# Query products on 64x64 float32 quarters, and attention steps done for two chunks at a time

## The chip, the cores and the metric

The kernel runs on one core of one Trainium2 chip. The metric is the device time of one execution in microseconds (us). Three executions of the kernel before were timed; a further one was profiled. The engines are named as the profile names them: PE is TensorE (matmuls), PEld its weight loads, DVE is VectorE, ACT is ScalarE, POOL is GpSimd, and SP is SyncE, whose queue starts nearly all DMAs here.

## What is computed

A linear attention without softmax, with an RMS norm, feeds two feed-forward layers. All arrays are float32 in the reference.

```
def _attn_ref(q, k, v, g_norm):                      # 8 batches, 8 heads, 576 rows, 64 wide
    kv = np.einsum('bhsd,bhse->bhde', k, v)
    out = np.einsum('bhsd,bhde->bhse', q, kv)
    rms = np.sqrt(np.mean(out * out, axis=-1, keepdims=True) + 1e-06)
    return out / rms * g_norm
x = transpose(attn, (0, 2, 1, 3)).reshape(4608, 512)
h = max(x @ w1, x @ w2, x @ w3)                      # 512 -> 768
x = h @ w_out                                        # 768 -> 512
h = x @ w_in                                         # 512 -> 2048
out = (s * relu(h)**2 + b) @ w_out2                  # 2048 -> 512
```

The weights of the first feed-forward layer reach the kernel as 64-bit floats, which it turns into float32 itself.

## The kernel before

**Stages.** The rows go through in nine groups of 512: the first 512 rows of each of the 8 batches, and as a ninth group the 64 left-over rows of all 8 batches. For group `j`, TensorE forms 18 sums of 12 matmuls each (`g1_part`, lines L96 to L98, PSUM tiles `g`), three for each of the 6 blocks of 128 hidden columns, whose maximum is kept; then 4 sums of 18 matmuls (`g2_mm`, the same lines, read `<-h,w_o`). The factor 12 is four chunks of 128 of the 512 columns, times three: a float32 matmul is done as three matmuls of split operands in fp32r (`mm3`). A split writes the high part on ACT (L92) and the low part, source minus high part, on DVE or POOL (L93). Attention of batch `j + 1` is worked out beside group `j`, so its matmuls stand between those of group `j`. Two Strassen-like stages for the second feed-forward layer follow from about 747 us on; the change does not touch them.

**Attention of a batch.** The 8 heads are handled in 4 pairs `p`: a pair is heads `p` and `p + 4`, one in partitions 0 to 63, the other in 64 to 127. `kv_mm` (L243) sums k times v for a pair in plain float32, into two halves of 64 PSUM partitions. `kv_diag` copies the sums into `kvf`, a 128x128 matrix for each pair with the two heads' 64x64 blocks on its diagonal and zeros elsewhere. `q_turn` transposes the pair's queries. `o_mm` multiplies: in batch 0 in one plain float32 matmul of 512 columns (L291), in the later batches in three fp32r matmuls (L295 to L297), for which `kv_diag` splits `kvf` and `q_split` the queries; one small float32 matmul of 64 columns (L300, tile `orps`) takes the left-over rows. `o_out` copies and squares the product (ACT); `ms_mm` sums the squares over a head (L325 in batch 0, L328 and L329 later, PSUM tile `ms`, one buffer); `ms_ln` takes ln, exp and a square on ACT; `ms_newton` does a Newton step of three DVE operations (L342 to L344); `x_split` splits the normalized chunk into `xh` and `xl`.

**The opening.** In group 0 nothing can be overlapped with an earlier group. The 18 blocks of w1 to w3 and 6 of w_out are loaded (`conv_load`, L149), turned to float32 (`conv_unpack`, `conv_sum`: L161 to L166 and L171, 3 operations on DVE, 3 on ACT, 1 on POOL) and split. Three staging buffers hold the raw blocks. The first four sums (`g` 0 to 3) of group 0 are formed chunk by chunk, as the chunks arrive.

**What sets the order.** Each step is entered with a position (`at(position, step, ...)`), and the steps are issued by position. From position 20 on, SP and PE keep that order; before it only SP does, and PE's order in the opening, like that of DVE, ACT and POOL all through, is set by a scheduler when the program is built. On the chip each engine works through its list strictly in order.

Of the kernel before, what the change touches and what calls it, by code (L numbers as in the profile page):

```python
# [9 lines left out]
F32 = mybir.dt.float32  # L10
F32R = mybir.dt.float32r
# [18 lines left out]
def attention_max_ffn_relu2_ffn(ctx: ExitStack, tc, q, k, v, g_norm, w1, w2, w3, wo, wi, w2o, s, b, out):  # L30
# [109 lines left out]

    st = {}
# [85 lines left out]
    def load_kv(bb, p):  # L227
        for nm, src in (("k", k), ("v", v)):
            tag = (nm, 2) if bb or p < 2 else ("o", NP)
            t = st[nm, bb, p] = at_.tile([P, 2, C, D], F32, tag=tag[0], bufs=tag[1], name=f"{nm}_{bb}_{p}")  # L230
# [3 lines left out]
    def kv_mm(bb, p):  # L234
        if p == 0:
            st["kvps", bb] = psa.tile([P, NP, D], F32, tag="kv", name=f"kvps_{bb}")
# [8 lines left out]
    def kv_out(bb):  # L245
        t = st["kvc", bb] = at_.tile([P, NP, D], F32, tag="kvc", bufs=4, name=f"kvc_{bb}")
        act(out=t, in_=st.pop(("kvps", bb)), func=AF.Copy)
# [6 lines left out]
    def kv_diag(bb):  # L254
# [9 lines left out]
        st["kvhl"] = (kvh, kvl)  # L264
# [15 lines left out]
    def q_split(bb, p):  # L280
        t = st["qt", p]
        qh = at_.tile([P, N], F32R, tag="qh", name=f"qh_{bb}_{p}")
        ql = at_.tile([P, N], F32R, tag="ql", name=f"ql_{bb}_{p}")
        split(qh, ql, t[:, :N], nc.vector)
        st["q", p] = (qh, ql)

    def o_mm(bb, p):
        ps = st["ops", p] = psa.tile([P, N], F32, tag="o", name=f"ops_{bb}_{p}")
        mm = nc.tensor.matmul
        if bb == 0:  # L290
            mm(ps, lhsT=kvf[:, p], rhs=st["qt", p][:, :N], start=True, stop=True)  # L291
        else:
            kvh, kvl = st["kvhl"]
            qh, ql = st["q", p]
# [3 lines left out]
        if p == 0:  # L298
# [580 lines left out]
```

## Time and profile before

| | us |
|---|---|
| three timed runs, median (lowest to highest) | 1456.11 (1453.32 to 1458.19) |
| profiled execution, first to last instruction | 1453.9 |
| PE busy in it | 1396.9 |
| DVE, ACT, POOL busy | 951.2, 813.8, 332.7 |
| group 0 (from the start to the first matmul of group 1) | 156.6 |
| groups 1 to 8 (to about 747 us) | 590 |
| the rest | 707 |

The profile gives no time of the profiled execution beyond its span. The span lies 2.2 us under the median of the timed runs and inside their spread of 4.9 us. PE's busy time counts a matmul from its start to a modelled end, so a row of matmuls without a gap shows as 100% busy; what one matmul costs in such a row is the step from its start to the next one's.

### The profile page before, as it was taken

The numbers are of one execution on the slowest core, as the hardware profiler recorded it, in microseconds if no ns is written. First come the engines' busy times: TensorE is split into PE (matmuls) and PEld (weight loads), VectorE is DVE, ScalarE is ACT, GpSimd is POOL, SyncE is SP. The second block draws the span as 40 slices with busy tenths as digits, with TensorE's granted clock in tenths as the row PEclk, the third lists the DMA queues.
The fourth block names the chain that finished last, engine by engine and source line by source line (L and its number), as shares of the span: only waits on it lengthen the run. The fifth ranks groups of instructions, "written<-read, shape, count | busy, mean of one in ns | idle before, by whom it ended". The sixth has DMA issues, their size and how long they took to land. (4 is left out here: it accounts for less than half of the span.)

```text
span 1453.9 us, 19580 instructions
## 1 busy us (share of the span) xinstructions
PE 1396.9 (96%) x6860; PEld 1145.0 (79%) x6860; DVE 951.2 (65%) x1439; ACT 813.8 (56%) x1454; POOL 332.7 (23%) x238
## 2 busy tenths in 40 slices
PE   4689999999999999999999999999999999999997
PEld 2467888888878788888878778988788888888887
DVE  4899473646364636446466765756877888888785
ACT  5776454445353545443365646647676666656565
POOL 1334242324232324331100000000002414141412
PEclk9789999999999999999999999999999999999999
DMA  9986244435364742213135464453676444454541
GB/s 195 198 207 106 76 65 111 111 117 102 127 91 124 113 123 58 80 29 116 65 124 202 162 230 178 142 203 127 217 265 231 132 146 174 152 175 148 176 135 40
DMA packets 229459, 202.63 MB, mean 139 GB/s; under 512 B 126320, under 2 KB 179568, under 8 KB 227184
## 3 DMA queue, kind: packets, MB, share of 16 engines
q1 hardware_dynamic: 229200, 201.11, 48.9%
q8 instruction: 54, 0.88, 0.3%
q14 instruction: 45, 0.37, 0.1%
q10 hardware_dynamic: 160, 0.26, 0.0%
HBM read 126.88 MB, written 74.45 MB: 138 GB/s over the span
## 5 line engine op out<-in xcount | busy, mean ns | idle before, releaser
L97 PE MATMUL g<-xl,w_w 128*128 128x512 f32 x648 | 255.9, 395 | 3.8 <-POOL xl L93 3.8
L96 PE MATMUL g<-xh,w_w 128*128 128x512 f32 x648 | 257.4, 400 | 0.2 <-ACT xh L92 0.2
L98 PE MATMUL g<-xh,w_w 128*128 128x512 f32 x648 | 255.6, 395 | 0.0
L92 ACT ACTIVATE zx<-z 128x512 fp32r<-128x512 f32 (+1 forms) x280 | 161.2, 586 | 123.5 <-PE zs_a L707 35.7
L629 PE MATMUL ps_a<-x_q,w_q 128*128 128x512 f32 (+1 forms) x960 | 211.1, 371 | 2.8 <-DVE cs L537 1.7
L707 PE MATMUL zs_a<-zx,w_q 128*128 128x512 f32 (+1 forms) x960 | 203.7, 369 | 0.6 <-POOL zx L93 0.3
L93 POOL TENSOR_TENSOR zx<-z,zx 128x512 fp32r<-128x512 f32 (+1 forms) x46 | 63.3, 1376 | 593.8 <-DMA gd<-cs 381.4
L629 PEld LDWEIGHTS ps_a<-x_q,w_q 128*128 128x128 f32 x960 | 167.2, 188 | 38.0 <-DVE cs L537 3.4
L93 DVE TENSOR_TENSOR zx<-z,zx 128x512 fp32r<-128x512 f32 (+1 forms) x234 | 170.6, 746 | 34.8 <-ACT zx L92 34.3
L707 PEld LDWEIGHTS zs_a<-zx,w_q 128*128 128x128 f32 x960 | 167.8, 188 | 31.9 <-POOL zx L93 0.7
L97 PEld LDWEIGHTS g<-xl,w_w 128*128 128x128 f32 x648 | 123.3, 190 | 29.7 <-POOL xl L93 4.2
L96 PEld LDWEIGHTS g<-xh,w_w 128*128 128x128 f32 x648 | 123.2, 191 | 26.8 <-issue 1.0
L98 PEld LDWEIGHTS g<-xh,w_w 128*128 128x128 f32 x648 | 123.2, 190 | 26.3
L171 POOL TENSOR_TENSOR tr_ctr<-tr_ctr,gc_cgc 128x512 int32<-128x512 int32 x42 | 56.0, 1333 | 232.4 <-DVE gc_cgc L166 169.8
L629 PE MATMUL ps_b<-x_q,w_q 128*128 128x512 f32 (+1 forms) x480 | 107.6, 372 | 1.1 <-ACT cs L640 1.0
L707 PE MATMUL zs_b<-zx,w_q 128*128 128x512 f32 (+1 forms) x480 | 103.8, 371 | 2.2 <-DVE zx L93 2.2
L372 DVE TENSOR_TENSOR h<-g,h 128x512 f32<-128x512 f32 x108 | 73.9, 684 | 42.9 <-PE g L98 42.4
L707 PEld LDWEIGHTS zs_b<-zx,w_q 128*128 128x128 f32 x480 | 83.9, 188 | 19.1 <-DVE zx L93 3.4
L629 PEld LDWEIGHTS ps_b<-x_q,w_q 128*128 128x128 f32 x480 | 83.8, 188 | 18.9 <-ACT cs L640 1.8
L96 PE MATMUL g<-h,w_o 128*128 128x512 f32 x216 | 85.7, 397 | 0.0
L162 ACT ACTIVATE tr_ctr<-raw_craw 128x512 int32<-128x512 uint32 x42 | 28.1, 669 | 102.1 <-DMA wd<-tr_ctr 86.1
L97 PE MATMUL g<-h,w_o 128*128 128x512 f32 x216 | 84.6, 392 | 0.0
(160 smaller groups left out, 2268.3 us busy)
## 6 DMA issues: line engine op xcount, KB each, us to landing
z<-gd SPq DMA_DIRECT2D x64, 512.0 KB
gd<-cs SPq DMA_DIRECT2D x96, 256.0 KB
z<-gd SPq DMA_DIRECT2D x48, 256.0 KB
x1d<-x SPq DMA_DIRECT2D x36, 256.0 KB
k<-in_k_dram SPq DMA_DIRECT2D x32, 256.0 KB
v<-in_v_dram SPq DMA_DIRECT2D x32, 256.0 KB
raw_craw<-in_moe_w_in_dram SPq DMA_DIRECT2D x16, 512.0 KB
wd<-tr_ctr SPq DMA_DIRECT2D x32, 256.0 KB
```

Of the source, the lines that this page charges most:

```text
L92: act(out=hi, in_=src, func=AF.Copy)
L93: eng.tensor_tensor(out=lo, in0=src, in1=hi.bitcast(F32), op=ALU.subtract)
L96: nc.tensor.matmul(ps, lhsT=w[:, 0, sl], rhs=xh, start=first, stop=False)
L97: nc.tensor.matmul(ps, lhsT=w[:, 0, sl], rhs=xl, start=False, stop=False)
L98: nc.tensor.matmul(ps, lhsT=w[:, 1, sl], rhs=xh, start=False, stop=last)
L162: act(out=r, in_=w32[:, :, 0], func=AF.Copy, scale=2.0 ** -29)
L171: nc.gpsimd.tensor_tensor(out=t, in0=t, in1=g.bitcast(I32), op=ALU.add)
L372: nc.vector.tensor_tensor(out=st["h", m], in0=ps, in1=st["h", m], op=ALU.max)
L629: nc.tensor.matmul(ps, lhsT=w[:, a, c], rhs=x[:, b_], start=new and k == 0 and e == 0, stop=k == HK - 1 and e == 2, skip_group_check=True)
L707: nc.tensor.matmul(ps, lhsT=w[:, a, c], rhs=x[:, b_, :n], start=new and k_ == 0 and e == 0, stop=k_ == 3 and e == 2, skip_group_check=True)
```

## The change

`o_mm` multiplies in plain float32 in all batches, on quarters of the array: for each head of a pair a 64x64 block of `kvf` is the stationary operand, with 64 partitions of queries. Two pairs, a unit `u`, share a PSUM tile of two banks: pair `2u` goes to output partitions 0 to 63 and pair `2u + 1` to 64 to 127, and the head decides the bank. A chunk now holds heads `4h + 2u` and `4h + 2u + 1`, so the blocks of w1 to w3 are loaded by one DMA of 128 partitions instead of two of 64, and chunks are taken in the order 0, 2, 1, 3 of the weights. The splits of queries and of `kvf` are gone. Copy, square, split of squares, the last two Newton operations and the split into `xh`, `xl` work on two chunks (1024 columns) at once; the sums of squares, ln, exp and the first Newton operation stay at 512. The left-over rows and the k-v sums share one PSUM bank (`kvor`). The low halves of chunks 0 and 1 in the opening move from POOL to DVE; in later groups POOL does the first unit's, DVE the second's.

```diff
     def w1_src(n):
-        return [(h * D, D, w[h * NP * D:(h + 1) * NP * D, :].rearrange("(k d) c -> d k c", d=D)) for h in range(2)]
+        return [(0, P, w.rearrange("(k p) c -> p k c", p=P))]
...
     def kv_diag(bb):
             act(out=kvf[sl, :, sl], in_=t[sl], func=AF.Copy)
-        if bb == 0:
-            return
-        kvh = at_.tile([P, NP, P], F32R, tag="kvh", name=f"kvh_{bb}")
-        kvl = at_.tile([P, NP, P], F32R, tag="kvl", name=f"kvl_{bb}")
-        split(kvh, kvl, kvf, nc.vector)
...
-    def q_split(bb, p):
-        split(qh, ql, t[:, :N], nc.vector)
-    def o_mm(bb, p):
-        ps = st["ops", p] = psa.tile([P, N], F32, tag="o", name=f"ops_{bb}_{p}")
-            mm(ps, lhsT=kvh[:, p], rhs=qh, start=True, stop=False)
-            mm(ps, lhsT=kvh[:, p], rhs=ql, start=False, stop=False)
-            mm(ps, lhsT=kvl[:, p], rhs=qh, start=False, stop=True)
-        mm(st["orps"][:, p], lhsT=kvf[:, p], rhs=st["qt", p][:, N:], start=True, stop=True)
+    def o_mm(bb, u, pp):
+        if pp[0] == 2 * u:
+            st["ops", u] = psa.tile([P, 2, N], F32, tag="o", name=f"ops_{bb}_{u}")
+        for h in range(2):
+            for p in pp:
+                sl = slice(h * D, (h + 1) * D)
+                nc.tensor.matmul(st["ops", u][p % 2 * D:(p % 2 + 1) * D, h], lhsT=kvf[sl, p, sl],
+                                 rhs=st["qt", p][sl, :N], start=True, stop=True)
+        for h in range(2):
+            for p in pp:
+                nc.tensor.matmul(kvor[p % 2 * D:(p % 2 + 1) * D, 1, 2 * u + h], lhsT=kvf[:, p, h * D:(h + 1) * D],
+                                 rhs=st["qt", p][:, N:], start=True, stop=True)
...
-    def ms_newton(bb, p):
-        stt(out=u, in0=st["ms", p], scalar=EPS, in1=u, op0=ALU.add, op1=ALU.mult)
+    def ms_newton(bb, c):
+        u = st["yu", c // 2][1][:, c % 2]
+        stt(out=u, in0=st["ms", c], scalar=EPS, in1=u, op0=ALU.add, op1=ALU.mult)
+    def o_norm(bb, u_):
         stt(out=u, in0=u, scalar=-3.0, in1=y, op0=ALU.add, op1=ALU.mult)
         stt(out=o, in0=o, scalar=g_sb, in1=u, op0=ALU.mult, op1=ALU.mult)
...
     for p in range(NP):
-        at(us(a + 2.7), o_out, 0, p)
-        at(us(a + 6), x_split, 0, p, nc.gpsimd if p < 2 else nc.vector)
+        if p % 2:
+            at(us(a + 2.7), o_out, 0, u)
+            at(us(a + 7), x_split, 0, u, nc.vector)
```

**The block in a later group.** PE's rows in batch 5's attention, between sums 12 and 13 of group 4, before: the product of one pair (`ops`) in three matmuls, the pair's left-over rows (`orps`) in one. There are four such blocks for a batch.

```order
L98 MATMUL g_4_12_3457<-xh_2997,w_w_698 128x512
L295 MATMUL ops_3_3479<-qh_3_3426,kvh_3173 128x512
L296 MATMUL ops_3_3479<-ql_3_3427,kvh_3173 128x512
L297 MATMUL ops_3_3479<-qh_3_3426,kvl_3174 128x512
L300 MATMUL orps_3238<-qt_3_3392,kvf 128x64
L96 MATMUL g_4_13_3495<-xh_2997,w_w_750 128x512
```

The same rows after, between sums 8 and 9 of group 4, for two pairs:

```order
L98 MATMUL g_4_8_3084<-xh_2761,w_w_521 128x512
L285 MATMUL ops_1_3107<-qt_2_3057,kvf 64x512
L285 MATMUL ops_1_3107<-qt_3_3082,kvf 64x512
L285 MATMUL ops_1_3107<-qt_2_3057,kvf 64x512
L285 MATMUL ops_1_3107<-qt_3_3082,kvf 64x512
L289 MATMUL kvor<-qt_2_3057,kvf 64x64
L289 MATMUL kvor<-qt_3_3082,kvf 64x64
L289 MATMUL kvor<-qt_2_3057,kvf 64x64
L289 MATMUL kvor<-qt_3_3082,kvf 64x64
L96 MATMUL g_4_9_3116<-xh_2761,w_w_543 128x512
```

Two blocks of four matmuls with 128 output partitions have become one block of eight with 64 each, and there are two such blocks for a batch.

**DVE in the opening.** DVE's rows around the low half of the last chunk of batch 0 (`xl<-o_3`), before. The tiles `gc`, `tr` and `raw` belong to the turning of weight blocks, `w_w` to their split.

```order
L165 SCALAR_TENSOR_TENSOR tr_o_586<-raw_o_547,tr_o_586 128x512
L161 TENSOR_SCALAR gc_o_621<-raw_o_570 128x512
L93 TENSOR_TENSOR kvl_556<-kvf,kvh_555 128x512
L166 SCALAR_TENSOR_TENSOR gc_o_587<-raw_o_547,tr_o_586 128x512
L93 TENSOR_TENSOR w_w_550<-tr_o_538,w_w_550 128x512
L93 TENSOR_TENSOR xl_292<-o_3_420,xh_291 128x512
L93 TENSOR_TENSOR w_w_577<-tr_ctr,w_w_577 128x512
L165 SCALAR_TENSOR_TENSOR tr_o_620<-raw_o_570,tr_o_620 128x512
```

The same place after; `raw_o_591` is the 14th block here, and `xl<-o_1` holds the low halves of chunks 2 and 3.

```order
L339 SCALAR_TENSOR_TENSOR o_1_389<-o_1_389,g_sb,u_1_428 128x1024
L167 SCALAR_TENSOR_TENSOR gc_cgc<-raw_craw,tr_ctr 128x512
L274 STREAM_TRANSPOSE qt_2_744<-qraw_398 128x576
L274 STREAM_TRANSPOSE qt_3_801<-qraw_398 128x576
L162 TENSOR_SCALAR gc_o_670<-raw_o_591 128x512
L308 TENSOR_SCALAR sqh_0_687<-sq_0_629 128x1024
L166 SCALAR_TENSOR_TENSOR tr_o_669<-raw_o_591,tr_o_669 128x512
L93 TENSOR_TENSOR xl_325<-o_1_389,xh_324 128x1024
```

Before, the block begun just ahead of the low half (`raw_o_570`) is the 12th, and the first operation on the 14th comes 12 rows behind the low half; now it comes 3 rows ahead of it. ACT's list has the same turn: the first ACT operation on the 14th block now stands directly ahead of the high halves of chunks 2 and 3.

**PE in the opening.** PE's rows after, from the k-v sums of batch 2 (`v_2_580`) to the first low-half matmul of chunks 2 and 3:

```order
L245 MATMUL kvor<-v_2_580,k_2_578 64x64 x8
L245 MATMUL kvor<-vrem,krem 64x64 x2
L285 MATMUL ops_1_863<-qt_2_744,kvf 64x512
L96 MATMUL g_0_0_342<-xh_324,w_w_183 128x512
L96 MATMUL g_0_1_349<-xh_324,w_w_211 128x512
L96 MATMUL g_0_2_356<-xh_324,w_w_254 128x512
L96 MATMUL g_0_3_363<-xh_324,w_w_276 128x512
L285 MATMUL ops_1_863<-qt_3_801,kvf 64x512
L285 MATMUL ops_1_863<-qt_2_744,kvf 64x512
L285 MATMUL ops_1_863<-qt_3_801,kvf 64x512
L245 MATMUL kvor<-v_3_614,k_3_612 64x64 x8
L97 MATMUL g_0_0_342<-xl_325,w_w_183 128x512
```

Ahead of that low-half matmul now stand all four k-v sums of batch 2 and all of batch 1's products. Before, one k-v sum of batch 2 and the product of one pair of batch 1 stood ahead of it; three k-v sums and nine fp32r matmuls of three pairs came later.

## Rows read from the trace of the kernel before

**Rows 1.** By stretch, us busy: PE, PEld, DVE, ACT, POOL; then clock, DMA share, GB/s.

```profile
0.00:156.60 156.60, 115.21 (x660) 84.70 (x661) 119.86 (x174) 101.33 (x181) 52.07 (x39) 0.88 0.81 165
156.60:747.00 590.40, 588.20 (x2858) 481.51 (x2858) 309.94 (x439) 280.87 (x480) 172.60 (x121) 1.00 0.40 96
747.00:1454.00 707.00, 693.52 (x3345) 578.80 (x3343) 521.35 (x827) 431.61 (x794) 108.02 (x78) 1.00 0.50 170
...
78.40:158.00 79.60, 71.14 (x407) 56.87 (x406) 68.49 (x94) 52.37 (x94) 30.31 (x19) 0.94 0.59 130
```

**Rows 2.** What PE waited for, 78 to 160 us: us, times, longest.

```profile
PE ms L328 <- DVE u L342: 3.4, 1, 3.4
PE kvps L243 <- DMA vrem<-in_v_dram: 3.2, 1, 3.2
PE kvps L243 <- DMA v<-in_v_dram: 1.9, 1, 1.9
```

**Rows 3.** PE: start, us, operation; last of the first four sums, first of group 1.

```profile
78.06 0.40 PE L98 MATMUL g<-xh,w_w 128*128 128x512 f32 x1
...
156.64 0.39 PE L96 MATMUL g<-xh,w_w 128*128 128x512 f32 x1
```

**Rows 4.** By stretch, columns as in rows 1: behind two of the waits.

```profile
104.00:108.00 4.00, 4.00 (x16) 2.83 (x17) 4.00 (x8) 3.52 (x7) 0.98 (x1) 0.57 0.84 302
134.00:142.00 8.00, 6.08 (x15) 4.78 (x16) 7.16 (x10) 4.18 (x7) 1.99 (x2) 0.57 0.64 107
```

**Rows 5.** PE in order of time: one pair's k-v sums between full matmuls.

```profile
528.30 0.39 PE L96 MATMUL g<-h,w_o 128*128 128x512 f32 x1
...
528.75 0.39 PE L98 MATMUL g<-h,w_o 128*128 128x512 f32 x1
529.07 0.69 PE L243 MATMUL kvps<-v,k 128*64 128x64 f32 x16
529.58 0.29 PE L243 MATMUL kvps<-vrem,krem 128*64 128x64 f32 x4
...
530.14 0.39 PE L97 MATMUL g<-xl,w_w 128*128 128x512 f32 x1
```

**Rows 6.** PE in order of time: one pair's products.

```profile
569.16 0.39 PE L295 MATMUL ops<-qh,kvh 128*128 128x512 f32 x1
...
569.85 0.33 PE L300 MATMUL orps<-qt,kvf 128*128 128x64 f32 x2
...
570.30 0.40 PE L97 MATMUL g<-xl,w_w 128*128 128x512 f32 x1
```

**Rows 7.** Tile ops: duration in ns (min/median/max), first and last start, form.

```profile
L295 PE MATMUL ops<-qh,kvh x28: 391/391/774, 70.4 to 569.2; 128*128 128x512 f32 x28
L291 PE MATMUL ops<-qt,kvf x8: 592/1061/1222, 9.3 to 35.9; 128*128 128x512 f32 x8
```

**Rows 8.** DVE's groups to 156.6 us: count, busy us, mean ns, idle before.

```profile
L93 DVE TENSOR_TENSOR ql<-qt,qh 128x512 fp32r<-128x512 f32 x5 | 4.2, 839 | 0.0
...
L93 DVE TENSOR_TENSOR kvl<-kvf,kvh 128x512 fp32r<-128x512 f32 x2 | 1.4, 678 | 0.0
```

**Rows 9.** Groups by form over the whole span: busy us, mean ns, idle before.

```profile
L537 DVE TENSOR_TENSOR cs<-ps_a,cs 128x512 f32<-128x512 f32 x32 | 21.6, 686 | 3.7 <-PE ps_a L629 3.6
...
L537 DVE TENSOR_TENSOR cs<-ps_a,cs 128x256 f32<-128x256 f32 x8 | 3.0, 418 | 0.2 <-PE ps_a L629 0.2
```

**Rows 10.** DVE and ACT in order of time: last low half; 14th block's start.

```profile
73.28 1.77 DVE L93 TENSOR_TENSOR xl<-o,xh 128x512 fp32r<-128x512 f32 x1
...
83.37 0.67 ACT L162 ACTIVATE tr_o<-raw_o 128x512 int32<-128x512 uint32 x1 [2.36 <-DMA raw_o<-in_moe_w_dram]
```

**Rows 11.** Tile raw_o, ns: SP's start of a 64-partition load; a block's first DVE operation.

```profile
L149 SPq DMA_DIRECT2D raw_o<-in_moe_w_dram x24: 595/608/733, 11.7 to 96.6; - x24
...
L161 DVE TENSOR_SCALAR gc_o<-raw_o x12: 410/427/1379, 17.1 to 102.8; 128x512 uint16<-128x512 uint16 x12
```

**Rows 12.** The page: the span.

```profile
span 1453.9 us, 19580 instructions
```

More of the change, by code (lines that the diff above doesn't have):

```diff
@@ L139, in attention_max_ffn_relu2_ffn @@
         nc.gpsimd.memset(rems[nm], 0.0)
+    kvor = psa.tile([P, 2, NP, D], F32, name="kvor")
     st = {}
@@ L324, in ms_mm @@
+    def ms_mm(bb, c):
+        u, h = divmod(c, 2)
+        ps = st["ms", c] = psa.tile([P, N], F32, tag="ms", name=f"ms_{bb}_{c}")
         if bb == 0:
-            nc.tensor.matmul(ps, lhsT=onesf, rhs=st["sq", p], start=True, stop=True)
+            nc.tensor.matmul(ps, lhsT=onesf, rhs=st["sq", u][:, h], start=True, stop=True)
             return
-        sqh, sql = st["sqhl", p]
-        nc.tensor.matmul(ps, lhsT=ones, rhs=sqh, start=True, stop=False)
-        nc.tensor.matmul(ps, lhsT=ones, rhs=sql, start=False, stop=True)
@@ L331, in ms_ln @@
-    def ms_ln(bb, p):
-        y = at_.tile([P, N], F32, tag="y", name=f"y_{bb}_{p}")
-        u = at_.tile([P, N], F32, tag="u", name=f"u_{bb}_{p}")
-        act(out=y, in_=st["ms", p], func=AF.Ln, bias=eps)
+        sqh, sql = st["sqhl", u]
+        nc.tensor.matmul(ps, lhsT=ones, rhs=sqh[:, h], start=True, stop=False)
+        nc.tensor.matmul(ps, lhsT=ones, rhs=sql[:, h], start=False, stop=True)
+    def ms_ln(bb, c):
+        u_, h = divmod(c, 2)
+        if h == 0:
+            st["yu", u_] = [at_.tile([P, 2, N], F32, tag=tg, name=f"{tg}_{bb}_{u_}") for tg in "yu"]
+        y, u = (x[:, h] for x in st["yu", u_])
+        act(out=y, in_=st["ms", c], func=AF.Ln, bias=eps)
@@ L402, in plan_norm @@
             at(t + u, sq_split, bb, p)
-        at(t + 3.3 * u, ms_mm, bb, p)
-        at(t + 4 * u, ms_ln, bb, p)
-        at(t + 6 * u, ms_newton, bb, p)
+        for c in range(2):
+            at(t + (3.3 + 2.7 * c) * u, ms_mm, bb, 2 * p + c)
+            at(t + (4 + 2.7 * c) * u, ms_ln, bb, 2 * p + c)
+            at(t + (5.6 + 2.7 * c) * u, ms_newton, bb, 2 * p + c)
+        at(t + 8.5 * u, o_norm, bb, p)
     T0 = -28 * US
@@ L430, in attention_max_ffn_relu2_ffn @@
         at(us(a - 0.5), q_turn, 0, p)
-        at(us(a + 2), o_mm, 0, p)
-        at(us(a + 2.7), o_out, 0, p)
-        plan_norm(0, p, us(a + 3), 0.4 * US)
-        at(us(a + 6), x_split, 0, p, nc.gpsimd if p < 2 else nc.vector)
-        for g in range(4):
-            at(us(a + 7.1) + 0.01 * g, g1_part, 0, g, [p])
-    at(us(24), o_rems, 0)
+        at(us(a + 2), o_mm, 0, p // 2, [p])
+        if p % 2:
+            u = p // 2
+            at(us(a + 2.7), o_out, 0, u)
+            plan_norm(0, u, us(a + 3), 0.4 * US)
+            at(us(a + 7), x_split, 0, u, nc.vector)
+            for g in range(4):
+                for c in range(2):
+                    at(us(a + 8.1) + 0.01 * g + 0.002 * c, g1_part, 0, g, [2 * u + c])
+    at(us(24.5), o_rems, 0)
     stages_o = [stages[0], stage(HS[M1 - 1], HS[M1 - 2], "st")]
```

95 lines of the change are left out of this document (40 added, 55 removed).

## Prediction

> **What bounds the kernel now.** I read the table by stretch first [rows 1]. From 156.6 us to the end PE is busy for 588.2 of 590.4 and 693.5 of 707 us at the full clock (2.4 GHz), while DVE is busy for half to three quarters and ACT for less. There the time is the sum of PE's steps, and a shorter or a longer operation on ACT or DVE is worth nothing as long as PE's operands come in time; the reader is to see that most of the elementwise work that the change saves lies here. The opening is different: in the first 156.6 us PE is busy for 115.2 at a mean clock of 0.88, and DVE for 119.9. So the change has two places to work: PE's blocks of query products in the later groups, and the opening. For the opening I then read what PE waits for behind its first four sums [rows 2, 3]: 3.4 + 3.2 + 1.9 = 8.5 us, and the stretches behind two of these waits [rows 4], where the clock of a share of the time is the low one (1.2 GHz): 0.57 on the mean is 0.86 low, so 3.4 of 4.0 and 6.9 of 8.0 us. Work takes double there. That costs 3.4 / 2 = 1.7 us in the first; in the second PE is idle for 8.00 - 6.08 = 1.9 us, of which 0.8 at least fall in the low part, and with 1.1 it is 5.8 / 2 = 2.9 us. Waits and low clock together cost 13.1 us between 78.4 and 156.6 us.
>
> **The blocks in the later groups.** In the row of fp32r matmuls two steps, 528.30 to 528.75, are 0.45 us [rows 5]. The three product matmuls of a pair take 569.16 to 569.85, which is 0.69 us; the small one takes what 569.85 to 570.30 holds beyond one step, 0.22 [rows 6]. Two pairs now cost 2 x 0.91 = 1.82 us.
>
> The new block is two float32 quarters for each pair. A float32 matmul shows as two records, and each of 512 columns is 592 - 391 = 0.20 us longer at best than an fp32r one, about one more pass of 512 columns at 2.4 GHz, 0.213 [rows 7]; so I take 2 x 0.213 = 0.43 us of streaming for a record and 0.85 for a quarter. Whether the four quarters of a unit run beside each other no row shows, since no operation of before uses 64 rows of the array. The nearest is the k-v sum, which uses two halves of 64 output columns: 16 records in 529.07 to 529.58, or 0.032 us each, where 64 columns in two passes need 0.053 in a row [rows 5]. Two halves do run beside each other. I take the same for rows, hence 0.85 us for the four; in turn they would take 3.4 (8 x 0.43), the other end. The small products are 8 records of the k-v kind, 8 x 0.032 = 0.26. The k-v block also shows the price of leaving and entering the full array: 528.75 to 530.14 is 1.39, less two steps it is 0.94, and 20 records of 0.032 are 0.64 of that, so 0.30 us. Between the 64-row quarters and the 128-row small products there is a further turn that no row shows; it costs between 0 and 0.30, and I take 0.15, since the array stays in halves of columns. Sum: 0.85 + 0.26 + 0.30 + 0.15 = 1.56, a gain of 0.26 us for a unit (0.11 to 0.41 by the further turn). Batches 2 to 7 have 12 units in the PE-bound part: **3.1 us** gained (1.3 to 4.9). The Trainium skill ("TensorEngine Tiling (Array Packing)", section Key Properties) says that tiles run independently, and that a change of tiling mode drains the array; the k-v row agrees with the first for columns, and its 0.30 us fits the second.
>
> The wait that could appear in these groups is that for `ms`, which has one buffer: the second chunk's sum waits until the first Newton operation on the first. PE's list holds 36 or more matmuls between them, 8.2 us and up, as before; I cost it at nothing, and 2 us if DVE is late in two batches.
>
> **The opening.** What is removed is work of DVE and ACT: five splits of queries and two of `kvf` on each before 156.6 us [rows 8], and the fixed part of each merged operation. From 686 and 418 ns for 512 and 256 columns a column costs 1.05 ns and the rest, 0.15 us, is fixed [rows 9], so a merged pair saves 0.15 us and takes 1.22. Seven operations of 0.69 and some ten merged pairs are 6.3 us, less 1.22 for the low halves that come from POOL: 5.1 of DVE's 119.9 us. That counts only where PE waits for DVE.
>
> What is moved weighs more. DVE and ACT now reach the 14th weight block before they split chunks 2 and 3. The 14th lands at 83.37 [rows 10]. If it lands then again, DVE has its first operation (0.43 [rows 11]), the split of squares (1.22 at most, I take 0.7), the second operation (0.69) and the low halves (1.22) to do, and chunks 2 and 3 are ready at 86.4 instead of 75 (73.28 + 1.77). PE then has 20 of the 24 matmuls for both chunks to do. It comes out of idling, and after such waits its clock was low [rows 4], with a step of 2 x 0.213 us; so 8.5 us, and the first four sums end at 95 instead of 78.4: 16.6 us later. Against that stands what was done meanwhile: three k-v sums of 0.94 and nine matmuls of 0.225, together 4.8 us, no longer come behind. And the 13.1 us of waits and low clock have lost their causes: the k-v data of batch 2 (1.9) and batch 3 (3.2) are long there when PE comes to them, and the `ms` wait (3.4) came from a DVE that was behind with weight blocks and query splits; at the end of the low halves it is now three weight blocks further (by its list, 12 weight splits stand ahead of them instead of 9). The load on SP is lighter by one start of 0.61 us for each block of w1 to w3 [rows 11]; the DMA engines are busy for 0.81 of the opening [rows 1], so of the first blocks' savings I count 1 us. Sum: 16.6 - 4.8 - 13.1 - 1 = **-2.3 us**. The bounds are wide: if none of the 13.1 comes back it is +10.8; if the 14th block comes 6 us earlier, because SP's starts were the limit, it is -8.3.
>
> **Sum.** -2.3 - 3.1 = -5.4 us. The span of the profiled execution is 1453.9 [rows 12], so its successor's should be 1448.5; the median of the timed runs is 2.2 us above the span, and I keep that distance: 1456.1 - 5.4 = **1450.7 us**.
>
> **Rivals.** 0.3% is 4.4 us, about what a measurement of this kernel can tell from no change; the three runs lie within 4.9.
>
> *Quarters not four at a time.* Each quarter's two records stand behind each other in PE's list, and the next quarter's first record behind both. If PE starts records strictly in that order, only the second record of one and the first of the next overlap: 5 x 0.43 = 2.15 instead of 0.85, and a block costs 2.86, 1.04 more than now. If columns pair but the two row halves take turns it is 4 x 0.43 = 1.72, a block of 2.43, 0.61 more. Over 14 units (batch 1's two as well) that is +8.5 to +14.6, with the opening +6 to +12: 1462 to 1468. For it: no row shows 64-row tiles; against it: 20 k-v records in 0.64 us. The Trainium skill ("TensorE: Matmul & The Clock Gate", Part 3) states strict program order for starts and ends of matmuls, which is the first of these cases; the same part also reports packed tiles that overlap fully, and the k-v row fits both.
>
> *The opening gets longer.* One mechanism: chunks 2 and 3 held behind the 14th block, without the later waits going away, because DVE still works through the remaining blocks at 2.5 us of work each (0.43 and three of 0.69) and the new first sums (`g` 4 and 5) wait for PSUM buffers that DVE frees only behind the 17th and 18th. With r of the 13.1 us recovered the total is 16.6 - 4.8 - 1 - r - 3.1 = 7.7 - r: slower than before below r = 7.7, clearly so below 3.3. With r = 1: 1463. For it: DVE is busy for 68.5 of the 79.6 us behind the first four sums [rows 1]; against it: its list has less work left at that point.
>
> *The opening pays more.* The block comes early and r is full: -8.3 - 3.1, 1445.
>
> *Nothing moves.* The further turn costs 0.30 or more, the opening comes out even: 1456.
>
> **How the numbers follow.** The forecast has a chance of 0.43, with a range of its own of 1446 to 1455 (0.31 of it beyond 4.4 us, 0.12 within). The opening that pays more: 0.12. Longer opening: 0.16 (0.13 slower, 0.03 within). Quarters not four at a time: 0.15 (0.12 slower, 0.03 within). Nothing moves: 0.14. So faster 0.43, same 0.32, slower 0.25. The range of 1441 to 1465 takes in both opening cases and the better half of the quarters' case; beyond it lie strict order (1468) and quarters one by one (1.56 + 2.6 a block, some +30 us), about 0.12.
>
> **What would show it.** In the later groups: the step from the last full matmul ahead of a unit's block to the second behind it, less two steps, is 1.56 us if four quarters run at once, 2.4 or 2.9 if not. The first four sums end at about 95 us, and the first matmul of group 1 starts at about 154; PE's waits between them fall from 8.5 to under 2 us. DVE and ACT are busy for less over the whole span without any of it showing in the time. The prediction is wrong if blocks cost more than 1.82, or if the 14th block lands much earlier or later than 83 us, or if waits for DVE's merged operations appear where none were.

## The result, and the profile after

The changed kernel is slower: 1465.97 us (1460.64 to 1468.00, six runs) against 1454.82 us (1452.38 to 1458.19, six runs) of the kernel before, a ratio of 1.0072 with an interval of 1.0059 to 1.0085. The forecast was 1450.7. The profiled execution has a span of 1464.2 us, 10.3 more than before [rows 12].

The windows of the changed kernel, columns as in rows 1: the opening, groups 1 to 8, the rest; then the stretch behind the first four sums; then stretches around waits in later groups.

```profile
0.00:155.00 155.00, 115.91 (x688) 79.40 (x689) 108.64 (x156) 97.42 (x162) 44.39 (x34) 0.93 0.70 166
155.00:742.30 587.30, 577.78 (x2873) 460.80 (x2872) 266.72 (x353) 249.24 (x395) 146.02 (x93) 0.99 0.38 94
742.30:1464.00 721.70, 706.74 (x3401) 589.26 (x3399) 530.50 (x843) 440.54 (x811) 108.21 (x78) 1.00 0.49 168
...
90.40:155.00 64.60, 61.47 (x339) 49.15 (x339) 49.18 (x66) 39.06 (x67) 18.98 (x12) 1.00 0.48 106
...
194.00:198.00 4.00, 1.70 (x7) 0.89 (x6) 2.40 (x3) 2.17 (x4) 3.57 (x2) 1.00 0.00 0
198.00:202.00 4.00, 4.00 (x12) 3.14 (x11) 2.45 (x3) 2.65 (x5) 1.59 (x1) 0.57 0.00 0
...
420.00:424.00 4.00, 1.99 (x8) 1.30 (x7) 2.85 (x4) 1.69 (x3) 3.53 (x2) 0.94 0.47 74
424.00:428.00 4.00, 4.00 (x13) 3.17 (x12) 2.41 (x3) 2.69 (x5) 1.60 (x1) 0.63 0.00 0
...
502.00:506.00 4.00, 4.00 (x12) 3.10 (x12) 3.35 (x3) 1.78 (x4) 1.57 (x2) 0.57 0.00 0
...
274.00:278.00 4.00, 4.00 (x20) 3.29 (x19) 0.91 (x3) 2.96 (x5) 1.30 (x1) 1.00 0.00 0
```

DVE's and ACT's busy time fell as forecast, and the opening ends at 155.0 us instead of 156.6. The loss is in the second line. In the kernel before, groups 1 to 8 end at 733.5 us; the 747 us named ahead of the prediction take in 13.5 us of the next stage. The same stretch before, up to that end:

```profile
156.60:733.50 576.90, 574.81 (x2802) 471.06 (x2802) 301.48 (x425) 272.62 (x465) 172.60 (x121) 1.00 0.40 96
```

So groups 1 to 8 took 576.9 us with 2.1 us of idle time on PE, and now take 587.3 with 9.5. What PE waits for there, 155 to 742.3 us, in the table of waits:

```profile
PE ms L319 <- DVE u L333: 8.0, 4, 2.7
PE ms L320 <- POOL sql L309: 1.4, 1, 1.4
```

In the kernel before, the same wait in groups 1 to 8:

```profile
PE ms L328 <- DVE u L342: 2.1, 2, 1.3
```

L319 is the first matmul of a sum of squares; L333 is the first Newton operation, which reads the previous sum for the last time and so frees the one buffer of `ms`.

PE in order of time: the end of the first four sums, the start of group 1, then group 4's second and third sum of squares with the last matmul ahead of the wait, and a unit's block in group 6.

```profile
90.04 0.39 PE L98 MATMUL g<-xh,w_w 128*128 128x512 f32 x1
...
155.02 0.39 PE L96 MATMUL g<-xh,w_w 128*128 128x512 f32 x1
...
411.73 0.39 PE L319 MATMUL ms<-sqh,ones 128*128 128x512 f32 x1
...
420.14 0.39 PE L98 MATMUL g<-xh,w_w 128*128 128x512 f32 x1
422.54 0.50 PE L319 MATMUL ms<-sqh,ones 128*128 128x512 f32 x1 [2.01 <-DVE u L333]
...
564.33 0.39 PE L98 MATMUL g<-xh,w_w 128*128 128x512 f32 x1
564.65 1.09 PE L285 MATMUL ops<-qt,kvf 64*64 64x512 f32 x8
565.67 0.45 PE L289 MATMUL kvor<-qt,kvf 128*64 128x64 f32 x8
566.05 0.50 PE L96 MATMUL g<-xh,w_w 128*128 128x512 f32 x1
566.39 0.40 PE L97 MATMUL g<-xl,w_w 128*128 128x512 f32 x1
```

The block is what the prediction named as its test: 564.33 to 566.39 is 2.06 us, less two steps 1.61, against a forecast of 1.56 and 1.82 before. So the loss is not in the quarters.

The other engines around the same wait, in order of time (the first four lines are from the opening and from group 1, for later):

```profile
77.04 0.67 ACT L163 ACTIVATE tr_o<-raw_o 128x512 int32<-128x512 uint32 x1
...
80.12 2.75 POOL L309 TENSOR_TENSOR sql<-sq,sqh 128x1024 fp32r<-128x1024 f32 x1 [0.97 <-DVE sqh L308]
...
80.56 3.38 DVE L93 TENSOR_TENSOR xl<-o,xh 128x1024 fp32r<-128x1024 f32 x1
...
215.91 2.59 DVE L93 TENSOR_TENSOR xl<-o,xh 128x1024 fp32r<-128x1024 f32 x1 [0.95 <-ACT xh L92]
...
413.90 0.78 DVE L274 STREAM_TRANSPOSE qt<-qraw 128x576 f32<-128x576 f32 x1 [3.23 <-DMA qraw<-in_q_dram]
...
417.49 0.66 ACT L163 ACTIVATE tr_ctr<-raw_craw 128x512 int32<-128x512 uint32 x1 [4.32 <-DMA wd<-tr_ctr]
...
419.76 0.68 ACT L327 ACTIVATE y<-ms,eps 128x512 f32<-128x512 f32 x1
...
421.79 0.69 DVE L333 SCALAR_TENSOR_TENSOR u<-ms,u 128x512 f32<-128x512 f32 x1 [1.12 <-ACT u L329]
```

The sum starts at 411.73. Its ln (L327) comes only at 419.76, because ACT's list has a weight block ahead of it, and ACT idles 4.32 us before that block's first operation. DVE too has waited 3.23 us for a transfer, but it is idle again for 1.12 us just ahead of Newton, until ACT is done: here ACT is the one that comes last. So Newton starts 10.1 us behind its sum. PE's list holds 38 records from one sum to the next, 8.6 us at a step of 0.226; the rest is the wait. Behind it PE's clock is the low one for a while: a mean of 0.57 is 0.86 low, 0.63 is 0.74, 0.94 is 0.12. That is 3.4 + 3.4 us in groups 1 and 5 and 3.4 (3.0 + 0.5) in group 4, where work takes double: 5.1 us lost. Behind the wait of 1.4 us in group 2 (the stretch from 274) the clock stays full.

**The sum of the difference.** Opening: 155.0 - 156.6 = -1.6. Groups 1 to 8: waits 9.4 - 2.1 = +7.3, low clock +5.1, twelve blocks at -0.21 = -2.5; together +9.9, where the stretches give 587.3 - 576.9 = +10.4. (By the lengths of whole groups, in the table under experiment 4, it comes out without a remainder.) The rest, which the change does not touch: 721.9 - 720.4 = +1.5; over all profiles of this study it takes 718.2 to 722.4.

### The profile page after: what moved, and what is told of

The parts are those of the page before. It is cut to its first block, busy times and chain, and to the rows that moved or that the text cites. A ratio compares the mean times of both kernels' runs of the same rounds, so it can differ in the third digit from the quotient of the medians.

```text
span 1464.2 us, 19476 instructions
## 1 busy us (share of the span) xinstructions
PE 1400.4 (96%) x6960; PEld 1129.5 (77%) x6960; DVE 905.9 (62%) x1351; ACT 787.2 (54%) x1367; POOL 298.6 (20%) x205
## 5 line engine op out<-in xcount | busy, mean ns | idle before, releaser
L162 DVE TENSOR_SCALAR gc_cgc<-raw_craw 128x512 uint16<-128x512 uint16 x42 | 22.8, 544 | 130.4 <-DMA raw_craw<-in_moe_w_in_dram 64.1
L96 PE MATMUL g<-h,w_o 128*128 128x512 f32 x216 | 85.5, 396 | 1.9 <-DVE h L369 1.9
```

Source lines behind the costliest of these rows:

```text
L96: nc.tensor.matmul(ps, lhsT=w[:, 0, sl], rhs=xh, start=first, stop=False)
L162: ts(out=c, in0=w16[:, :, 3], scalar1=0x7FFF, scalar2=None, op0=ALU.bitwise_and)
```

## The experiments

Each was timed beside the kernel before on the same chip, three chips in all; ratios are to that, 95% intervals in brackets, and the changed kernel's is 1.0072. The kernel before had medians of 1451.4 to 1454.8 us in these measurements, so different versions are compared by ratio; what was expected is mostly on the scale of the result above (1454.8 and 1466.0). "Distance" is the number of PE's records from the start of a group's second sum of squares to that of the third.

**1. Sums later.** In the changed kernel, the second unit's sums stand one sum of `g` later; in group 7 the spacing of sums is 3 of `g` instead of 2.

```diff
-                plan_norm(bb, u, a + 3.9, 0.9)
+                plan_norm(bb, u, a + 3.9 + (u if j else 0), 0.9)
...
-                plan_norm(B, u, a + 0.5, 0.9)
+                plan_norm(B, u, a + 0.5, 1.1)
```

> The changed kernel with the two sums of squares of a group's second unit one sum of g (12 matmuls, 2.7 us) later in PE's list, with the work behind them; in group 7 the two sums of a unit three sums of g apart instead of two. Distance theory: in the changed kernel a sum of squares stands 38 matmuls (8.6 us) behind the one ahead of it (26 in group 7), and the Newton operation that frees the single buffer comes up to 10.7 us behind its sum; so PE idles 9.4 us in groups 1, 2, 4, 5 and 7, and the low clock behind three of these waits costs another 4.8. With 50 matmuls (11.3 us) the waits fall below 1 us and the low stretches go: about 13 us less, 1453. Rival, lateness travels: Ln and Newton move back with their sums, or the second unit is then late for the next group's first sum: a wait of the old size stands elsewhere, 1460 to 1466.

1447.53 us, ratio 0.9974 (0.9962 to 0.9986): faster than both kernels. The table of waits in groups 1 to 8, and DVE's low halves of the second unit in group 1, for later:

```profile
PE g L96 <- ACT h L367: 0.8, 1, 0.8
PE ms L319 <- DVE u L333: 0.2, 1, 0.2
...
215.61 1.23 DVE L93 TENSOR_TENSOR xl<-o,xh 128x1024 fp32r<-128x1024 f32 x1 [1.13 <-ACT xh L92]
```

The windows, as above:

```profile
154.20:726.90 572.70, 571.70 (x2874) 457.57 (x2874) 271.78 (x355) 250.94 (x397) 151.11 (x93) 1.00 0.39 97
```

The waits and the low clock are gone with nothing else changed in what is computed. The lateness did not travel, but for 1.6 us in group 5, most of it where `g` now waits for its own buffer. Newton is as late as ever (9.4, 10.3 and 12.1 us behind the second sum in groups 1, 4 and 5); 50 records, 11.3 us, just leave room for it.

**2. Merged work cut in halves.** From batch 2 on, the operations of 1024 columns are two of 512 again; PE's list is that of the changed kernel.

```diff
+    def halves(bb):
+        return [slice(0, 1), slice(1, 2)] if bb > 1 else [slice(0, 2)]
...
-        act(out=o, in_=st["ops", u], func=AF.Copy)
+        for c in halves(bb):
+            act(out=o[:, c], in_=st["ops", u][:, c], func=AF.Copy)
```

(and so for square, split of squares, the last two Newton operations and the split into `xh`, `xl`)

> The changed kernel with the merged operations (copy, square, split of squares, the last two Newton operations, split into xh and xl) cut into their two halves of 512 columns from batch 2 on; quarters, sums and PE's list stay. Merged-work theory: the 1024-column operations (1.0 to 2.4 us each) hold Ln and Newton up on ACT, DVE and POOL, so with halves the waits at the sums fall to the 2 us of the kernel before: about 1454. Distance theory: Newton is late because it and Ln stand behind weight blocks that wait for their transfer, and the sums are 38 matmuls apart either way; only the 1.4 us wait for POOL's low half in group 2 goes: 1463 to 1466, more if the extra fixed parts delay something.

1460.23 us, ratio 1.0058 (1.0045 to 1.0071). Its waits in groups 1 to 8:

```profile
PE ms L325 <- DVE u L339: 7.4, 4, 2.7
```

POOL's part is gone and the rest stays, Newton at 10.4, 9.6 and 10.7 us behind the second sum in groups 1, 4 and 5: the length of the merged operations is not what makes it late. Their place in the lists stayed as it was.

**3. The kernel before with sums closer.** The third and fourth chunk's sums one sum of `g` earlier.

```diff
-                plan_norm(bb, p, a + 4.5, 0.9)
+                plan_norm(bb, p, a + 4.5 - (j > 0 and p > 1), 0.9)
```

> The kernel before with the sums of squares of the third and fourth chunk of a group one sum of g earlier in PE's list, so that the third stands 31 matmuls (7.0 us) behind the second instead of 43 (9.7 us). Distance theory: Newton on the second chunk comes 10.3 and 9.8 us behind its sum in groups 4 and 5, so the third sum waits 3.3 and 2.8 us there (1.3 and 0.8 before), each with a low-clock stretch of 1.6 us behind it; in groups 1 to 3 it comes 5.6 to 7.2 us behind, no more than 0.2 of wait. 4.0 of more waiting and 3.2 of clock: 7 us slower than the kernel before, 1462. Rival: the distance is not what decides, Newton follows its neighbours: within 2 us of the kernel before.

1472.69 us, ratio 1.0134 (1.0116 to 1.0152). Its waits in groups 1 to 8:

```profile
PE ms L328 <- DVE u L342: 14.1, 6, 4.7
```

The sign is right and the size too small: the expectation miscounted, since the block of a pair no longer lies between the two sums and the distance is 26 records, 5.9 us. The kernel before, without any part of the change, loses more than the change cost once its sums stand this close, which is closer than the changed kernel's 38. Not all of the 14.1 us is distance alone: in group 1 it is the fourth sum that waits, 2.2 us, 43 records behind the third, because the third's Newton now comes 11.4 us behind its sum.

**4. The kernel before with sums later.** A first try moved them by a whole sum of `g`; the last chunk's split then stood ahead of its last Newton operation, so that this part of the norm is left out of what it splits. The second moved them by 0.7 in the plan, which is the same place in PE's list and keeps the norm.

```diff
-                plan_norm(bb, p, a + 4.5, 0.9)
+                plan_norm(bb, p, a + 4.5 + (0.7 if j and p > 1 else 0), 0.9)
```

> The kernel before with the sums of squares of the third and fourth chunk of each later group one sum of g (12 matmuls) further back in PE's list, the same remedy that the version with sums later had for the changed kernel. Distance theory: the two waits of 1.3 and 0.8 us in groups 4 and 5 go, 2 us less than the kernel before: ratio 0.9985, and what the change itself is worth, both kernels having the remedy, is the rest to 0.9974, that is 1 to 3 us. Rival, the later sums cost the kernel before something of their own (its high and low halves of the last chunk are then late for the next group): ratio 1.000 or above.

> The kernel before with the third and fourth chunk's sums of squares one sum of g later again, moved only so far that the last chunk's split still stands behind its norm (the earlier try left that norm out of the split). Distance theory: the waits in groups 4 and 5 go, their periods fall from 76.5 and 76.0 to 74.9 us, the others stay: ratio 0.998 to 0.999 to the kernel before, so that the changed kernel with its remedy (0.9974) is still ahead by the blocks (3.2 us). Rival: the last chunk's halves are late for the next group's first sum: waits for xh or xl there, ratio above 1.

1452.66 us, 0.9997 (0.9986 to 1.0008), and 1450.55 us, 0.9993 (0.9980 to 1.0005). Both profiles show no wait of PE in groups 1 to 8, and periods of 74.9 us in groups 4 and 5. The gain in the time, 0.4 and 1.0 us by the ratios, can't be told from nothing, and in the second not from the 2 us of waits either. Against it, the changed kernel with the same remedy (0.9974) is ahead by about 3 us, the size of the blocks; that is little more than these intervals can tell. From the first matmul of a group to that of the next, in us:

| group | 1 | 2 | 3 | 4 | 5 | 6 | 7 |
|---|---|---|---|---|---|---|---|
| before | 71.1 | 74.8 | 74.9 | 76.5 | 76.0 | 71.2 | 67.2 |
| before, sums later (second try) | 71.1 | 74.8 | 74.9 | 74.9 | 74.9 | 71.2 | 67.2 |
| changed | 75.0 | 76.2 | 74.4 | 78.3 | 78.9 | 70.7 | 68.6 |
| changed, sums later | 70.5 | 74.2 | 74.4 | 74.4 | 76.0 | 70.7 | 67.2 |

Where neither kernel waits, a group is 0.54 us shorter with the change: the two blocks, 0.27 each. Six groups have them: 3.2 us. What the waits cost with all that follows them can be read here too, without a model of the clock, against the rows with sums later (in group 5 of the changed kernel 74.4, as in groups 3 and 4): 4.5 + 2.0 + 3.9 + 4.5 + 1.4 = 16.3 us in the changed kernel's groups 1, 2, 4, 5 and 7, and 1.6 + 1.1 = 2.7 before. 16.3 - 2.7 - 3.2 = +10.4 us is what the stretches gave.

**5. Both heads' quarters on the same rows**, and **6. full-array float32 products**, both on the version with sums later, from batch 2 on.

```diff
-                nc.tensor.matmul(st["ops", u][p % 2 * D:(p % 2 + 1) * D, h], lhsT=kvf[sl, p, sl],
-                                 rhs=st["qt", p][sl, :N], start=True, stop=True)
+                r = slice(0, D) if bb > 1 else sl
+                nc.tensor.matmul(st["ops", u][p % 2 * D:(p % 2 + 1) * D, h], lhsT=kvf[r, p, r],
+                                 rhs=st["qt", p][r, :N], start=True, stop=True)
```

> The version with sums later, and from batch 2 on both heads' quarters read the same 64 partitions (the first head's block of kvf and the first head's queries), so the second head's product is left out and its place is filled with the first's. Theory: four quarters run beside each other because they use four different parts of the array; now two of them share each part, so the quarters take 1.96 us instead of 0.98 and a block 2.6 instead of 1.6: 12 x 0.98 = 12 us more than the version with sums later (1447.5), 1459. Rival: the quarters are cheap by themselves and the overlapping starts in the records say nothing: block 1.6, no change.

```diff
+        if bb > 1:
+            for p in pp:
+                nc.tensor.matmul(st["ops", u][:, p % 2], lhsT=kvf[:, p], rhs=st["qt", p][:, :N],
+                                 start=True, stop=True)
```

> The version with sums later, and from batch 2 on one plain float32 matmul of 128x128 for a pair instead of two quarters; the chunks then hold other heads than their weight blocks, so the numbers that come out are of another pairing, the work has the same size. Theory: two full float32 matmuls are four records of 0.43 us in a row, 1.72 us instead of 0.98 for four quarters, so a block is 2.3 us and 12 units cost 8 to 9 us more: 1456. Rival: a full float32 matmul costs no more than the quarters (0.2 us above an fp32r one for each record at best): within 2 us of 1447.5.

1458.75 us, 1.0040 (1.0027 to 1.0054), and 1458.81 us, 1.0038 (1.0025 to 1.0051): both lose the 0.3% that the version with sums later had gained, and 0.4% more. No wait of PE appears in their groups 1 to 8. A block in group 6, same rows:

```profile
557.53 0.39 PE L98 MATMUL g<-xh,w_w 128*128 128x512 f32 x1
557.85 1.93 PE L286 MATMUL ops<-qt,kvf 64*64 64x512 f32 x8
559.71 0.45 PE L290 MATMUL kvor<-qt,kvf 128*64 128x64 f32 x8
...
560.43 0.39 PE L97 MATMUL g<-xl,w_w 128*128 128x512 f32 x1
```

And the full array:

```profile
558.80 0.40 PE L98 MATMUL g<-xh,w_w 128*128 128x512 f32 x1
559.04 1.88 PE L284 MATMUL ops<-qt,kvf 128*128 128x512 f32 x4
560.85 0.45 PE L293 MATMUL kvor<-qt,kvf 128*64 128x64 f32 x8
...
561.57 0.39 PE L97 MATMUL g<-xl,w_w 128*128 128x512 f32 x1
```

From the quarters' start to that of the small products it is 1.86 us with two quarters on each part of the array, 1.02 with one (564.65 to 565.67), and 1.81 for four full records. So the four quarters do run beside each other, because they lie on four parts. The blocks are 2.45 and 2.32 us where 2.6 and 2.3 were expected.

**7. Chunks early in the opening**, on the changed kernel. The split's new plan position stands ahead of the last two Newton operations of batch 0, which are so left out of what it splits; the first four sums then wait neither for the 14th block nor for that part of the norm.

```diff
-            at(us(a + 7), x_split, 0, u, nc.vector)
+            at(us(a + 6), x_split, 0, u, nc.vector)
```

> The changed kernel with the splits of the opening's chunks one place earlier in the plan (7 to 6), so that the high and low halves of the last two chunks stand ahead of the 8th weight block on ACT and DVE instead of behind the 14th. Prediction's theory of the opening: what ends the first four sums late is the 14th block, but what PE does meanwhile does not come behind; so the first four sums end 5 to 10 us earlier (80 to 85 us instead of 90), and the first matmul of group 1 moves by less than 3 us (155.0 in the changed kernel): 1463 to 1467. Rival, the late chunks cost the opening what they are late: group 1 starts 5 to 10 us earlier, 1456 to 1461.

1455.56 us, ratio 1.0027 (1.0014 to 1.0039). PE: the end of the first four sums, and the first matmul of group 1:

```profile
55.28 0.40 PE L98 MATMUL g<-xh,w_w 128*128 128x512 f32 x1
...
152.48 0.39 PE L96 MATMUL g<-xh,w_w 128*128 128x512 f32 x1
```

The first four sums end 34.8 us earlier, more than expected, and group 1 starts only 2.5 earlier: what PE does first in this opening hardly moves its end. The time is 6.5 us below the changed kernel's by the ratios, which is where the rival had it, though not for the rival's reason: 2.5 is the opening, group 1 is 1.9 shorter (73.1 instead of 75.0; its wait of 1.9 us was followed by no low clock) and group 7 1.4 (67.2 instead of 68.6; its wait is gone). Why those waits changed is not explained.

**8. Two loads for a weight block**, on the version with sums later.

```diff
-        return [(0, P, w.rearrange("(k p) c -> p k c", p=P))]
+        return [(h * D, D, w.rearrange("(k p) c -> p k c", p=P)[h * D:(h + 1) * D]) for h in range(2)]
```

> The version with sums later, with each block of w1 to w3 loaded by two DMAs of 64 partitions again instead of one of 128, same rows. Prediction's step: SP is lighter by a start of 0.61 us for each block, and of that 1 us counts in the opening: group 1 starts at about 155 us instead of 154.2, 1448.5. Rival, starts on SP were the opening's limit: the first 14 blocks land up to 8 us later and group 1 starts at 158 or later: 1452 or more. Rival, the DMA engines are the limit and the starts are hidden: no change.

1457.51 us, ratio 1.0032 (1.0020 to 1.0044): by the ratios 8 us above the version with sums later, for a term that the prediction put at 1. ACT's first operation on the 14th block and PE's first matmul of group 1 (76.00 and 154.24 in the version with sums later, 77.04 and 155.02 in the changed kernel):

```profile
82.15 0.68 ACT L163 ACTIVATE tr_o<-raw_o 128x512 int32<-128x512 uint32 x1 [2.47 <-DMA raw_o<-in_moe_w_dram]
...
163.46 0.39 PE L96 MATMUL g<-xh,w_w 128*128 128x512 f32 x1
```

The first rival holds: the 14th block is 6.2 us later. The scheduler orders the opening anew for slower loads, so the 9.2 us from 154.2 to 163.46 are the loads and the order that follows from them together.

**9 to 12. Which transfer makes Newton late.** The queries of batches 3 to 7 are loaded later, behind a weight block instead of ahead of it (on the changed kernel, then on the version with sums later), or earlier (on both).

```diff
-            at(max(t - 10, us(20)), load_q, bb, 0, NP)
+            at(t - 7.4 if j > 1 else max(t - 10, us(20)), load_q, bb, 0, NP)
```

and for earlier:

```diff
-            at(max(t - 10, us(20)), load_q, bb, 0, NP)
+            at(t - 13.5 if j > 1 else max(t - 10, us(20)), load_q, bb, 0, NP)
```

> The changed kernel with the queries of batches 3 to 7 loaded 2.6 sums of g later, so that in groups 1 to 5 SP starts the weight block that then stands ahead of the second Ln on ACT before the queries instead of behind them; sums stay 38 matmuls apart. Cause theory: Newton is late because ACT and DVE wait for that block's transfer; it lands some 7 us earlier (SP is busy from 401.9 to 408.8 us with the starts of the queries), Newton on the second chunk comes less than 8.6 us behind its sum, and the waits in groups 4 and 5 go with their low clock: 7 us less than the changed kernel there, 5 to 10 in all: 1453 to 1458. Rival: what holds the block is its buffers (the one ahead of it must be stored first), not the start: no change, 1463.

> The version with sums later and the queries loaded later, both. Its waits are gone already but for some 1.6 us in group 5, where g waits for a buffer that ACT and DVE free behind a weight block. Cause theory: these go as well: 1 to 2 us below the version with sums later, ratio 0.996 to 0.997. Rival: the later queries hold up the next group's products: above 0.998.

> The changed kernel with the queries of batches 3 to 7 loaded 3.5 sums of g (9.5 us) earlier instead of 2.6 later; sums stay 38 apart. Transfer theory: in group 4 Newton stands on DVE behind the turning of these queries (waits 3.2 us for them) and its Ln on ACT behind a weight block that waits 4.3 us for the store of the block ahead, which SP starts behind the queries; with the queries out of the way both come earlier, the waits in groups 4 and 5 (2.0 and 2.7 us) fall below 1 us with their low clock, 1455 to 1459 if nothing else is late. Rival: some other transfer takes the place, as when they were loaded later: waits of 8 us or more in all, 1461 to 1466.

> The version with sums later and the queries loaded earlier, both. Distance theory: with 50 matmuls between the sums it no longer matters for the sums which transfer is late; only the 1.6 us in group 5, where g waits for a buffer, can go: ratio 0.996 to 0.998. Rival: the earlier queries collide with other loads: above 0.998.

Queries later on the changed kernel: 1465.18 us, 1.0094 (1.0075 to 1.0113). The cause theory falls. Its waits in groups 1 to 8, in the table of waits:

```profile
PE ms L319 <- DVE u L333: 12.1, 4, 4.6
```

DVE in group 4 shows why:

```profile
425.60 1.44 DVE L274 STREAM_TRANSPOSE qt<-qraw 128x576 f32<-128x576 f32 x2 [4.51 <-DMA qraw<-in_q_dram]
426.96 0.65 DVE L333 SCALAR_TENSOR_TENSOR u<-ms,u 128x512 f32<-128x512 f32 x1
```

ln now comes in time (4.2 us behind its sum), but on DVE Newton stands behind the turning of the queries, and those are late instead. Queries earlier: 1462.98 us, 1.0078 (1.0060 to 1.0096), 9.6 us of waits in the same table:

```profile
PE ms L319 <- DVE u L333: 9.2, 5, 3.1
PE ms L320 <- POOL sql L309: 0.4, 1, 0.4
```

Some transfer is late either way, as the rival had it. With sums later, the same two edits give 1450.91 us, 0.9996 (0.9984 to 1.0009), and 1449.68 us, 0.9981 (0.9970 to 0.9992): no wait for `ms` in groups 1 to 8 in either, only 1.4 and 1.0 us for buffers of `g`. By size that is the rival's side in both, the second only by a hair, and neither is faster than the version with sums later as it was. With the queries later the kernel before is no longer beaten, with them earlier it is. In the profiles the three hardly differ in groups 1 to 8 (572.6, 573.9, 573.4 us); they differ in the opening (154.2, 155.0, 157.5).

All of it in one table (in group 7 of the changed kernel, and of those built on it without moving its sums, two sums stand 26 apart):

| kernel | distance | PE's waits for `ms`, groups 1 to 8, us | ratio |
|---|---|---|---|
| before, sums closer | 26 | 14.1 | 1.0134 |
| changed, queries later | 38 | 12.1 | 1.0094 |
| changed, queries earlier | 38 | 9.6 | 1.0078 |
| changed | 38 | 9.4 | 1.0072 |
| changed, halves | 38 | 7.4 | 1.0058 |
| changed, chunks early | 38 | 7.8 | 1.0027 |
| before | 43 | 2.1 | 1 |
| changed, sums later | 50 | 0.2 | 0.9974 |
| changed, sums later, queries either way | 50 | 0 | 0.9996, 0.9981 |
| before, sums later | 55 | 0 | 0.9993 |

The versions of experiments 5, 6 and 8 stand 50 apart and don't wait for `ms` either; their 1.0040, 1.0038 and 1.0032 come from the dearer blocks and from the opening.

## Why the prediction was wrong

**The step that failed** is the sentence on the wait for `ms`: "PE's list holds 36 or more matmuls between them, 8.2 us and up, as before; I cost it at nothing". Where Newton is late it was not as before. In the old list the small block of a pair lay between a group's second and third sum, 43 records or 9.7 us; the new unit's block lies ahead of both, so 38 are left, 8.6 us, and 26 in group 7. (38 were there before too, but between the third sum and the fourth and in group 7, where Newton comes at most 6.6 us behind.) The other side of the comparison was not read at all: how long Newton takes to come. In the trace of before it starts 10.3 and 9.8 us behind the second sum in groups 4 and 5 (410.82 to 421.13 and 487.28 to 497.09), which already gave the two waits there:

```profile
410.82 0.39 PE L328 MATMUL ms<-sqh,ones 128*128 128x512 f32 x1
...
421.13 0.69 DVE L342 SCALAR_TENSOR_TENSOR u<-ms,u 128x512 f32<-128x512 f32 x1 [0.25 <-ACT u L336]
...
487.28 0.39 PE L328 MATMUL ms<-sqh,ones 128*128 128x512 f32 x1
...
497.09 0.69 DVE L342 SCALAR_TENSOR_TENSOR u<-ms,u 128x512 f32<-128x512 f32 x1
```

A margin that is used up was taken for a margin. The price of "2 us if DVE is late" left out the clock: 9.4 us of waits and 5.1 of low clock behind three of them. Experiments 1 and 3 show this from both sides. The list is not the whole of the 9.4 us: five records more, 1.0 us in the trace of before (9.6 against 8.6), would have left 1.2, 1.0 and 1.7 of the 2.2, 2.0 and 2.7 us and 0.4 of the 1.4, and twelve more in group 7 nothing of its 1.1 (an estimate from these rows). Of the 4.3 us that it leaves, 2.1 were there before; the rest is Newton, or POOL's low half, coming later in groups 1, 2 and 5.

**Blocks** were right: 1.61 us where 1.56 was forecast, and 3.2 us over the six groups by experiments 1 and 4 where 3.1 was. Their parts were less right than their sum, which is in part luck: the four quarters take 1.02 us for 0.85, the small products 0.38 for 0.26, and the steps into and out of the block, beyond a usual step, 0.09 and 0.11 for 0.45 of turns. The rival of quarters that take turns is out, by experiment 5, and so is strict order record by record, which needed 2.15 us for the quarters. The Trainium skill ("TensorE: Matmul & The Clock Gate", Part 3) says that packed tiles start about 4 ns apart and overlap; in the trace the first four records of a block start within 20 ns of each other, 6 to 7 ns apart, and the second four 0.48 us behind the first, so the trace agrees on the overlap.

**Opening.** The total of -2.3 is near the -1.6 of the one profile, but that is luck. Among the profiles of this study with the changed opening (the changed kernel, experiments 1, 2, 5, 6 and 9 to 12) group 1 starts at 153.0 to 157.6, 155.4 on the mean; among those with the old one at 155.0 to 156.6, mean 155.7. So the opening gained nothing that can be told. Its terms were mis-sized and cancelled. The 14th block comes to ACT at 77.04 instead of 83.37 [rows 10], 6.3 us earlier, where the lighter load on SP was counted with 1; two loads again put it back to 82.15, and group 1 to 163.46. For a block 6 us earlier the prediction had the bound of -8.3, and that was not reached. The low halves behind the block, counted with 1.22 us, took 3.38 (80.56 to 83.94). The first four sums end at 90.0, not 95: 12.0 later than before [rows 3]; their last 20 matmuls began at 85.59 and ran at steps of 0.23 us, the full clock, where 0.43 had been counted. The waits behind them did fall, to 3.0 us with the clock at 1.00, but from there to group 1 only 13.6 us were made up, where 4.8 + 13.1 = 17.9 had been counted. With two loads group 1 starts 6.8 us later than in the kernel before, as in "the opening gets longer"; whether by that rival's mechanism is not shown.

**ACT and DVE** are busy for less (905.9 and 787.2 us for DVE and ACT, before 951.2 and 813.8), without a gain in time, as said. The length of the merged operations did not cause the lateness either, by experiment 2, apart from the 1.4 us in group 2 that PE waits for POOL's merged low half: a wait where none was, as the prediction's last sign of being wrong has it.

**Open** is which transfer, or which of ACT's and DVE's lists, one would have to change so that Newton comes in time. Group 1 shows it plainest: Newton comes 5.6 us behind the second sum before and 10.2 after. There ACT's list can be read: ahead of the ln stand the weight block's three operations in both kernels, begun at 191.55 and followed by the ln at 193.50 before; after, they begin at 189.25 and the ln comes at 194.22, without a gap, because the second unit's copy and square (2.0 us), copies of k-v sums and one of `h` stand between them. No experiment moved these. Moving the queries either way only changed which transfer it waits behind.

## What to carry to other kernels

Where a result has one buffer, compare two times before a list is moved: how long the consumer takes to free the buffer, at its worst in the trace, and how much work the producer's list holds until the next use. A wait of 1 us in the trace says that the margin is gone, so that every instruction taken out from between costs nearly in full (17 records, 3.8 us, in experiment 3, where the longest wait went from 1.3 to 4.7), and the low clock that can follow comes on top (here 5.1 us behind 6.9 us of waits). A faster block is best tested with the spacing restored: here the same change is 0.7% slower or 0.3% faster by the place of two sums in a list.

## What the runs showed of the hardware

- Waits of only 2.2, 2.0 and 2.7 us were each followed by 4 us with a mean granted clock of 0.57 to 0.63, so mostly the low one; behind waits of 1.4 and 1.1 us, and of 1.3 and 0.8 in the kernel before, the clock stayed full. Between them it went either way: full behind waits of 1.6 and 1.9 us in experiments 2 and 7, low for a part of the time behind one of 1.85 in experiment 3 (means of 0.72 and 0.85 in two stretches of 4 us).
- Eight float32 records on four quarters of 64x64 take 1.02 us, and four on the full array, with the same useful products, 1.81.
- The low halves of two chunks on DVE, 128x1024 with two operands in SBUF, took 1.23 us in each of six groups with sums later, where POOL had no work beside them (215.61 in group 1), and 2.58 to 2.59 in each of six groups of the changed kernel, where POOL worked at the first unit's (215.01 to 217.42 in group 1); in the opening 3.38 at 80.56, with POOL at work from 80.12 to 82.87. It is not always DVE that pays: at 51.74 the same operation took 1.23 us although POOL began an addition at 51.99, and that one took 2.11 where the median of its kind is 1.29. The Trainium skill ("GPSIMD Engine Reference", the table's row on SBUF interfaces) says that GpSimd shares its SBUF interfaces with VectorE, and that there is contention with DVE instructions that have two SBUF inputs; the trace agrees, without showing the interface itself.
- Starting one DMA of 128 partitions instead of two of 64 for each weight block brought ACT's first operation on the 14th block 6.2 us earlier (76.00 against 82.15 us, both with sums later), with the bytes unchanged and with the order that the scheduler then chose.
